# The last block of a cosformer attention + MLP kernel: its first product by seven block products, its units set between halves of the tails' second product

## The chip, the cores and the metric

The kernel runs on one core of a Trainium2 chip. A core has TensorE (PE, with its weight loads as PEld), VectorE (DVE), ScalarE (ACT), GpSimd (POOL) and SyncE (SP), each with a queue of its own, a memory SBUF of 128 partitions, and PSUM, in which TensorE leaves its sums: eight banks of 512 f32 columns. The metric is the time of one execution in microseconds (us) as the device takes it, here the median of a few runs.

## The reference

```python
def phi(x, c, s):
    r = np.maximum(x, 0.0)
    return np.concatenate([r * c, r * s], axis=-1)
q_p, k_p = phi(q, cos_w, sin_w), phi(k, cos_w, sin_w)
kv = np.einsum('bhsf,bhsd->bhfd', k_p, v)
z = np.sum(k_p, axis=2)
num = np.einsum('bhsf,bhfd->bhsd', q_p, kv)
den = np.einsum('bhsf,bhf->bhs', q_p, z)[..., None] + 1e-06
x = (num / den).transpose(0, 2, 1, 3).reshape(B * S, H * D)
h = x @ w_in
g = h * (1.0 / (1.0 + np.exp(-1.702 * h)))
out = g @ w_out
```

q, k and v have 8 batches, 8 heads, 576 positions and 64 features; w_in is 512 x 2048, w_out 2048 x 512. So x has 4608 rows of 512 columns. The function of h is called gelu below; ACT has it as one operation.

## The kernel before

**Blocks.** One batch is a block, b from 0 to 7 (`B` is 8). Its 576 rows of x are 512 main rows, in `x[b]` (columns of x on the partitions in four chunks `kc`, rows along the free axis), and 64 tail rows, which all blocks gather in one tile `xt`. gelu of the main rows goes to four tiles `gT[0..3]` of a pool with five buffers, each with four groups `fc` of 128 columns of h; that of the tails goes to `gt`. The first product h = x @ w_in is made for one `fc` at a time: `mm1` runs four matmuls of 512 columns into one bank of the PSUM pool `pmm` (four buffers of a bank) and ACT's gelu reads it. `wcol(kc, fc)` is the weight: 128 of the columns of w_in with a stride of four. `mm1_tails(fc)` does the same for the 448 tail rows of blocks 1 to 7 together, once, at the end.

**The second product** g @ w_out runs by Winograd's form of Strassen's scheme: rows, the 2048 inner columns and the 512 output columns are cut in two each, and seven block products (`PRODUCTS`, in the order p1 p2 p6 p5 p7 p3 p4) take the place of eight. Each is two halves c of eight matmuls of 256 columns. Three banks are used: w, x and y. p1, p6, p7 and p4 accumulate in x one upon the other, so between two of them x must have been read: p1 and p6 are copied out by ACT (`keep`), p7 is added to the kept p5 on DVE (`join`). p2 goes to w, p5 and p3 to y. The sums of blocks of g (`g_sums`: s1 to s4, each in two calls h of 128x1024) are made on DVE, those of w_out lie ready in `wsum`. For the tails the sums lie in `kr` and `qT`, free by then.

**A block of the loop** (b from 1 on): the 16 `fc` of the first product; meanwhile DVE makes the next block's operands from q, k and v (`trig_q`, two halves for each of five chunks, each chunk then turned by a DMA from SP's queue, `qturn_dma`; `kv_operands`, two `trig` halves for each of nine j, cosine and sine, and a copy of v), and the sums of g. In block 1 the sine halves of the odd j for block 2 are ACT's. At `fc` 14 the next block's kv is made. Then the second product, between whose halves `x_next(nb, c)` makes one chunk of the next block's x: eight matmuls (`num_mm`) into a tile of the PSUM pool `pat` (two buffers of two banks, tile name "at"), three DVE operations (`num_div`: den, inv, xn), and a DMA transpose from SP's queue into `x[nb]` or, for chunk 4, `xt`.

**The last block** (7) has nothing to prepare. Before, it runs: the main rows' first product (L365, gelu L371), `mm1_tails` for all 16 `fc` (L396, gelu L398), the tails' sums and their second product (L507), then the main rows' second product, for which `wino_open(last=True)` gives bank x as two banks, one for each half, and `wino_last` copies and stores each half of p4 by itself. The results of the tails go out by 16 DMAs (`tail_out`), on SP and POOL by turns, those of the main rows by SP.

**Order.** The program is under manual scheduling: each engine's queue holds its instructions in the order in which the code issues them, and an engine waits at an instruction until what it needs has been signalled.

## Time and profile before

| | us |
|---|---|
| median of three runs (281.71 to 282.14) | 281.97 |
| the profiled execution | 282.08 |
| its span, first to last instruction | 280.3 |

The span by stages, from the table of windows (busy time of each engine; the granted TensorE clock is 1.00 in each):

| stage | from, to | PE | DVE | ACT |
|---|---|---|---|---|
| block 6, first product | 197.6, 213.0 | 15.40 | 13.24 | 9.60 |
| block 6, second product | 213.0, 226.2 | 13.20 | 8.99 | 2.35 |
| block 7, main first product | 226.2, 240.0 | 13.80 | 3.46 | 9.55 |
| block 7, tails' first product | 240.0, 252.1 | 12.10 | 3.46 | 8.75 |
| block 7, both second products | 252.1, 276.7 | 24.60 | 8.09 | 5.45 |

A line of the timeline gives start, length, engine, line of the code, operation, what is written from what, shape and count, and in brackets the idle time before it with what ended it. A line of groups gives count, busy time and the mean of one in ns. A line of the chain gives start, length and what the end of the execution waited for then. The length of a matmul in these lines includes the passage through the array; the pace is the start of one to the start of the next.

### The profile page before, as it was taken

To read this page: it belongs to the slowest core of one execution; us is meant where nothing else is said; L and a number is where in the kernel's file an instruction comes from. 1 tells how busy PE (TensorE), PEld (TensorE's weight loads), DVE (VectorE), ACT (ScalarE), POOL (GpSimd) and SP (SyncE) were. 2 spreads that over 40 slices of the span, in tenths; PEclk is the share of its full clock that TensorE was granted. 3 is DMA by queue.
4 is the path that set the end of the run, shared out by engine and by line. 5 is a ranking of instruction groups with operands and counts; after the bars stand their busy time and mean duration, and the time that the engine had idled before them with its cause. 6 is when DMAs were issued, how large, how long until landed. Compare 5 with 4: busy or idle time off the path is not lost.

```text
span 280.3 us, 6580 instructions
## 1 busy us (share of the span) xinstructions
PE 271.2 (97%) x2700; PEld 190.0 (68%) x2700; DVE 184.5 (66%) x450; ACT 130.6 (47%) x230; POOL 41.4 (15%) x70
## 2 busy tenths in 40 slices
PE   7899999999989999999999999999999999999994
PEld 2685645847965588558955895589658965568884
DVE  4843676786893986987598759875987612416111
ACT  6967552677116511652166215621562146772221
POOL 5690002300130012100110012002200120000320
PEclk9999999999999999999999999999999999999999
DMA  7999999999789998999799979968991430000243
GB/s 236 250 210 298 275 281 163 342 325 187 198 147 370 165 205 225 316 170 202 203 324 173 196 187 366 178 183 134 370 221 22 103 112 2 0 0 2 54 135 112
DMA packets 73661, 53.57 MB, mean 191 GB/s; under 512 B 52736, under 2 KB 63488, under 8 KB 73632
## 3 DMA queue, kind: packets, MB, share of 16 engines
q1 hardware_dynamic: 67504, 36.97, 59.8%
q0 software_dynamic: 6128, 16.19, 20.9%
q8 instruction: 21, 0.34, 0.6%
q14 instruction: 8, 0.07, 0.1%
HBM read 36.70 MB, written 9.44 MB: 165 GB/s over the span
## 4 chain that ended last, share of the span: by engine, by line
PE 81%; DMA 11%; DVE 4%; SPq 1%; ACT 1%; issue 1%; POOL 0%; DVEq 0%
PE mm L507 34%; PE mm L365 31%; DMA kf<-in_k_dram 8%; PE mm L396 4%; PE mm L419 4%; PE at L237 3%; PE at L310 3%; DMA sums<-in_v_dram 2%; DVE kr L169 2%; PE mm L388 1%; PE mm L205 0%; ACT kr L167 0%; DVE vt L193 0%; SPq L219 0%; DVE sums L474 0%
## 5 line engine op out<-in xcount | busy, mean ns | idle before, releaser
L365 PE MATMUL mm<-xT,w_in 128*128 128x512 bf16 (+1 forms) x592 | 113.9, 349 | 1.6 <-DMA xT<-xn 1.2
L371 ACT ACTIVATE g<-mm 128x512 bf16<-128x512 f32 x128 | 75.1, 598 | 38.9 <-PE mm L365 38.9
L365 PEld LDWEIGHTS <-w_in 128*128 128x128 bf16 x592 | 60.1, 113 | 48.6 <-issue 2.1
L507 PEld LDWEIGHTS <-sums 128*128 128x128 bf16 x448 | 42.3, 98 | 4.7
L513 POOL DMA_DIRECT2D out_dram<-ysb x24 | 17.5, 729 | 158.3 <-DVE inv L323 96.1
L507 PE MATMUL mm<-wsum,sums 128*128 128x256 bf16 x336 | 40.1, 272 | 0.0
L507 PEld LDWEIGHTS <-g 128*128 128x128 bf16 x336 | 32.2, 98 | 3.8
L169 DVE TENSOR_SCALAR kr<-kf,cosw 128x256 bf16<-128x256 f32 x69 | 23.8, 350 | 9.8 <-DMA kf<-in_k_dram 9.8
L325 DVE TENSOR_TENSOR xn<-at,inv 128x512 bf16<-128x512 f32 x39 | 27.0, 691 | 1.3
L507 PE MATMUL mm<-w_out_sb,g 128*128 128x256 bf16 x224 | 26.4, 272 | 0.0
L169 DVE TENSOR_SCALAR kr<-kf,sinw 128x256 bf16<-128x256 f32 x64 | 21.7, 339 | 0.0
L522 ACT ACTIVATE kept_p<-mm 128x512 f32<-128x512 f32 (+1 forms) x17 | 9.7, 572 | 21.5 <-PE mm L507 21.4
L185 DVE TENSOR_SCALAR qn<-qf,cosw 128x512 bf16<-128x512 f32 (+1 forms) x33 | 16.3, 494 | 2.2 <-DMA qf<-in_q_dram 2.2
L522 ACT ACTIVATE kept_u<-mm 128x512 f32<-128x512 f32 (+1 forms) x9 | 4.9, 550 | 26.7 <-DVE xn L325 16.8
L574 ACT ACTIVATE ysb<-mm 128x512 f32<-128x512 f32 x6 | 3.6, 598 | 29.5 <-PE mm L507 29.5
L310 PEld LDWEIGHTS <-qT 128*128 128x128 bf16 x312 | 14.3, 97 | 3.3 <-issue 1.0
L310 PE MATMUL at<-kvs,qT 128*128 128x65 bf16 x312 | 15.7, 193 | 0.8 <-DVE kvs L245 0.8
L321 DVE TENSOR_SCALAR den<-at 128x8 f32<-128x8 f32 x36 | 5.9, 163 | 15.8 <-PE at L310 15.8
L185 DVE TENSOR_SCALAR qn<-qf,sinw 128x512 bf16<-128x512 f32 (+1 forms) x33 | 15.6, 473 | 0.0
L474 DVE TENSOR_TENSOR sums<-g 128x1024 bf16<-128x1024 bf16 x14 | 9.2, 681 | 8.8 <-ACT g L371 8.8
L470 DVE TENSOR_TENSOR sums<-g 128x1024 bf16<-128x1024 bf16 x14 | 9.6, 687 | 7.9 <-ACT g L371 7.8
L419 PE MATMUL mm<-w_out_sb,g 128*128 128x512 bf16 x64 | 14.8, 379 | 0.0
(120 smaller groups left out, 266.2 us busy)
## 6 DMA issues: line engine op xcount, KB each, us to landing
kf<-in_k_dram SPq DMA_DIRECT2D x6, 1152.0 KB, 6.6
vf<-in_v_dram SPq DMA_DIRECT2D x6, 1152.0 KB, 11.4
qf<-in_q_dram SPq DMA_DIRECT2D x6, 1024.0 KB, 6.8
out_dram<-ysb POOLq DMA_DIRECT2D x24, 256.0 KB, 6.7
w_out_sb<-in_moe_w_out_dram POOLq DMA_DIRECT2D x4, 512.0 KB, 17.5
kf<-in_k_dram POOLq DMA_DIRECT2D x1, 1152.0 KB, 13.4
vf<-in_v_dram POOLq DMA_DIRECT2D x1, 1152.0 KB, 20.6
w_in<-in_moe_w_in_dram POOLq DMA_DIRECT2D x2, 512.0 KB, 10.1
```

The costliest lines, as they stand in the source:

```text
L169: eng.tensor_scalar(o, i, 0.0, w[:, j:j + 1], op0=MAX, op1=MUL)
L185: nc.vector.tensor_scalar(o, i, 0.0, sc, op0=MAX, op1=MUL)
L310: nc.tensor.matmul(ps[:, h // 4, ds((h % 4) * 65, 65)], qT[:, h, ts(c, 128)], kvs_of(h), start=not eps_too, stop=(not eps_too or h % 4 == ...
L325: nc.vector.tensor_tensor(xn, pv[:, :, :, 0:64], inv.unsqueeze(3).to_broadcast([128, 2, 4, 64]), op=MUL)
L365: nc.tensor.matmul(hp[fc][:, t0:t1], wcol(kc, fc), x[b][:, kc, t0:t1], start=(kc == 0), stop=(kc == KC - 1))
L371: nc.scalar.activation(gT[fc // 4][:, fc % 4], hp.pop(fc), AF.Gelu_apprx_sigmoid)
L396: nc.tensor.matmul(hps[:, 64:B * 64], wcol(kc, fc), xt[:, kc, 64:B * 64], start=(kc == 0), stop=(kc == KC - 1))
L419: nc.tensor.matmul(yp[b, t, c0][:, c0:c1], w, w_out_sb[:, fc, c0:c1], start=(fc == 0), stop=(fc == FC - 1))
L470: tt(o[n], a_blk(1, h), a_blk(1, h + 2), op=ADD)
L507: nc.tensor.matmul(bank[to][c], lhs, rhs, start=opens, stop=(fc == HF - 1), skip_group_check=True)
L513: eng.dma_start(out=dst[:, 2 * i + c0:2 * i + c1, ts(n, HD)], in_=t[:, c0:c1])
L522: nc.scalar.activation(o, i, AF.Identity)
```

## The change

It touches block 6, whose work prepares block 7, and block 7.

In block 7 the first product too runs by the same seven block products, for all main rows, and for half of the `fc` of the tails. x is cut in two by columns (k) and by rows (t), w_in by its rows (k) and its columns (f: `fc` 0 to 7 and 8 to 15). A `Unit` makes two `fc` of either half of f: seven products of four matmuls, 256 columns wide for the main rows (w = 0), 224 for the tails (w = 1). Its steps p come in the order 1 2 6 7 5 4 3 and use three banks: A for p1, p6, p7 and p4, one upon the other, Bk for p2, Bp for p5 and p3. p1, p6 and p7 are copied from A to SBUF (`snap`; by ACT in main units, by DVE in tail units), and DVE adds one of these to p2, p5 or p3 (`add`), whose result gelu reads from SBUF; p4's gelu reads A.

The eight banks are laid out by hand as `P8`: 0 to 3 are four tiles of `pmm`, 4 and 5 the halves of one tile of `pat`, 6 and 7 those of another. The tails come first: units of `fc` 0, 1, 8, 9 and of 4, 5, 12, 13 with A in P8[4] and P8[5], Bk P8[6], Bp P8[7], each with four of the other `fc` as `mm1_tails` between its steps, in P8[0..3]. Then four main units, A alternating between P8[4] and P8[5], Bp between P8[7] and P8[3], with three halves of the tails' second product between the steps of each (its w, x, y are P8[1], P8[0], P8[2]), then the two halves left, then the main second product with w P8[6], x P8[4] and P8[5], y P8[7].

The sums of w_in (`win_sum`, s1 to s4, two calls each) are made on DVE in block 6, s1 and s2 after `kv_operands(7)`, s3 and s4 between the chunks of x; those of the tails' x (`x_sum(1, ...)`) after the last chunk, those of the main x after the first tail unit. They lie in kf, vf and qf, the copies and adds in qn, all free by then. Four of the ten `trig_q` halves for block 7 (chunks 3 and 4) and the sine halves of its odd j go from DVE to ACT.

```diff
-    def mm1_tails(fc):
-        hps = pmm.tile([128, MT], F32, name="mm")
+    def mm1_tails(fc, hps):
         for kc in range(KC):
             nc.tensor.matmul(hps[:, 64:B * 64], wcol(kc, fc), xt[:, kc, 64:B * 64],
                              start=(kc == 0), stop=(kc == KC - 1))
...
-    def wino_open(last=False):
+    banks = {"main": {}, "tail": {}}
+
+    def use(which):
+        bank.clear()
+        bank.update(banks[which])
+
+    def give(which, w, x, y):
+        for n, t in (("w", w), ("x", x), ("y", y)):
+            one_bank = not isinstance(t, tuple)
+            two = [t.rearrange("p (c d) -> p c d", c=2)[:, c] for c in range(2)] if one_bank else [
+                u[:, 0:HD] for u in t]
+            banks[which][n] = two
+            banks[which][n, "all"] = t.rearrange("p (c d) -> p c d", c=2) if one_bank else None
+
+    def wino_open():
         for n in ("w", "x", "y"):
-            if last and n == "x":
-                two = [pmm.tile([128, 512], F32, name="mm") for _ in range(2)]
-                bank[n] = [t[:, 0:HD] for t in two]
-                bank[n, "all"] = None
-            else:
-                t = pmm.tile([128, 2, HD], F32, name="mm")
-                bank[n] = [t[:, c] for c in range(2)]
-                bank[n, "all"] = t
+            t = pmm.tile([128, 2, HD], F32, name="mm")
+            bank[n] = [t[:, c] for c in range(2)]
+            bank[n, "all"] = t
...
+    ws = {}
+    for t, names in ((kf, ("s1", "s2")), (vf, ("s3", "s4"))):
+        both = t.rearrange("p i e -> p (i e)")[:, 0:2048].bitcast(BF16).rearrange(
+            "p (n k f) -> p n k f", n=2, k=2)
+        for i, n in enumerate(names):
+            ws[n] = both[:, i]
+    xs_all = qf[:, 0:2048].bitcast(BF16).rearrange("p (w n k t) -> p w n k t", w=2, n=4, k=2)
+    xs = [{n: xs_all[:, w, i] for i, n in enumerate(("t3", "t1", "t2", "nt4"))} for w in range(2)]
+    slots = [qn.rearrange("p c h f -> p (c h f)").bitcast(F32)[:, ts(i, 512)] for i in range(5)]
+    slots.append(qf[:, 2048:2560])
+    slot_no = [0]
+
+    def slot(n):
+        slot_no[0] += 1
+        return slots[slot_no[0] % 6][:, 0:2 * n].rearrange("p (f t) -> p f t", f=2)
+
+    def win_sum(n, i):
+        tt = nc.vector.tensor_tensor
+        o = {m: ws[m][:, :, ts(i, 512)] for m in ws}
+        a = {(0, k): w_in_t[i][:, ts(k, 2), :] for k in range(2)}
+        a.update({(1, k): w_in_t[2][:, ts(k, 2), ts(i, 512)] for k in range(2)})
+        if n == "s1":
+            tt(o[n], a[1, 0], a[1, 1], op=ADD)
+        elif n == "s2":
+            tt(o[n], o["s1"], a[0, 0], op=SUB)
+        elif n == "s3":
+            tt(o[n], a[0, 0], a[1, 0], op=SUB)
+        else:
+            tt(o[n], a[0, 1], o["s2"], op=SUB)
+
+    def x_blk(w, b, k, t):
+        if w == 0:
+            return x[b][:, ts(k, 2), ts(t, 256)]
+        return xt[:, ts(k, 2), 64:B * 64].rearrange("p k (b a t) -> p k a b t", a=2, t=32)[:, :, t]
+
+    def x_sum(w, b, n):
+        tt = nc.vector.tensor_tensor
+        o = dict(xs[w])
+        if w:
+            o = {m: o[m][:, :, 0:(B - 1) * 32].rearrange("p k (b t) -> p k b t", t=32) for m in o}
+        if n == "t3":
+            tt(o[n], x_blk(w, b, 1, 1), x_blk(w, b, 0, 1), op=SUB)
+        elif n == "t1":
+            tt(o[n], x_blk(w, b, 0, 1), x_blk(w, b, 0, 0), op=SUB)
+        elif n == "t2":
+            tt(o[n], x_blk(w, b, 1, 1), o["t1"], op=SUB)
+        else:
+            tt(o[n], x_blk(w, b, 1, 0), o["t2"], op=SUB)
+
+    class Unit:
+        def __init__(self, w, b, u, A, Bk, Bp, act):
+            self.w, self.b, self.u, self.act = w, b, u, act
+            self.n = 256 if w == 0 else (B - 1) * 32
+            self.A, self.Bk, self.Bp = [t[:, 0:2 * self.n].rearrange("p (f t) -> p f t", f=2)
+                                        for t in (A, Bk, Bp)]
+
+        def mm(self, to, a, t, opens):
+            for j in range(2):
+                fc = 2 * self.u + j
+                for k in range(2):
+                    if isinstance(a, str):
+                        lhs = ws[a][:, k, ts(fc // 4, 512)].rearrange("p (f c) -> p f c", c=4)[:, :, fc % 4]
+                    else:
+                        lhs = wcol(2 * a[1] + k, 8 * a[0] + fc)
+                    if isinstance(t, str):
+                        rhs, o = xs[self.w][t][:, k, 0:self.n], to[:, j]
+                    else:
+                        rhs, o = x_blk(self.w, self.b, *t)[:, k], to[:, j]
+                        if self.w:
+                            o = o.rearrange("p (b t) -> p b t", t=32)
+
+                    nc.tensor.matmul(o, lhs, rhs, start=(opens and j == 0 and k == 0), stop=(k == 1),
+                                     skip_group_check=True)
+
+        def g_of(self, f, t):
+            if self.w:
+                return gt5[:, ds(8 * f + 2 * self.u, 2), t, 1:B].rearrange("p f b t -> p f (b t)")
+            return gT[2 * f + self.u // 2][:, ds(2 * (self.u % 2), 2), ts(t, 256)]
+
+        def gelu(self, f, t, i):
+            nc.scalar.activation(self.g_of(f, t), i, AF.Gelu_apprx_sigmoid)
+
+        def add(self, i, j):
+            o = slot(self.n)
+            nc.vector.tensor_tensor(o, i, j, op=ADD)
+            return o
+
+        def snap(self, i):
+            o = slot(self.n)
+            if self.act:
+                nc.scalar.activation(o, i, AF.Identity)
+            else:
+                nc.vector.tensor_copy(o, i)
+            return o
+
+        def step(self, p):
+            if p == 1:
+                self.mm(self.A, (0, 0), (0, 0), True)
+                self.s1 = self.snap(self.A)
+            elif p == 2:
+                self.mm(self.Bk, (0, 1), (1, 0), True)
+                self.gelu(0, 0, self.add(self.s1, self.Bk))
+            elif p == 6:
+                self.mm(self.A, "s2", "t2", False)
+                self.s2 = self.snap(self.A)
+            elif p == 7:
+                self.mm(self.A, "s3", "t3", False)
+                self.s3 = self.snap(self.A)
+            elif p == 5:
+                self.mm(self.Bp, "s1", "t1", True)
+                self.gelu(1, 1, self.add(self.s3, self.Bp))
+            elif p == 4:
+                self.mm(self.A, (1, 1), "nt4", False)
+                self.gelu(1, 0, self.A)
+            else:
+                self.mm(self.Bp, "s4", (1, 1), False)
+                self.gelu(0, 1, self.add(self.s2, self.Bp))
...
     def kv_operands(b):
         for j in range(NS):
-            trig(kr, kf, j, act="sin" if b == 2 and j % 2 else False)
+            trig(kr, kf, j, act="sin" if b in (2, B - 1) and j % 2 else False)
         if b > 2:
             vcopy()
...
     for b in range(1, B):
         nb = b + 1 if b + 1 < B else None
+        if nb is None:
+            break
         f0 = 5 if b == 1 else 0
         for fc in range(f0, FC):
             if nb is not None and fc == f0:
                 for c in range(5):
-                    trig_q(c)
+                    trig_q(c, act=(nb == B - 1 and c > 2))
                     qturn_dma(c)
             if nb is not None and fc == f0 + 1 and b > 1:
                 kv_operands(nb)
+                if nb == B - 1:
+                    for n in ("s1", "s2"):
+                        for i in range(2):
+                            win_sum(n, i)
 
...
                         x_next(nb, c2)
                         if c2 == 3 and nb + 1 < B:
                             load_kv(nb + 1)
+                        if nb == B - 1 and c2 in (1, 2):
+                            win_sum("s3", c2 - 1)
+                        if nb == B - 1 and c2 in (3, 4):
+                            win_sum("s4", c2 - 3)
+                        if nb == B - 1 and c2 == 4:
+                            for n in ("t1", "t2", "t3", "nt4"):
+                                x_sum(1, nb, n)
...
-            continue
-        for fc in range(FC):
-            mm1_tails(fc)
-            if fc == 0:
-                g_sums(("s1", "s2", "s4"), 1)
-        for h in range(2):
-            g_sums(("s1", "s2"), h, TAIL)
-        g_sums(("s3",), 0, TAIL)
-        g_sums(("s3",), 1, TAIL)
-        wino_open()
-        for p in range(7):
-            for c in range(2):
-                wino_mm(p, c, TAIL)
+
+
+
+    b = B - 1
+    two = [pat.tile([128, 2, 512], F32, name="at") for _ in range(2)]
+    P8 = [two[i // 2][:, i % 2] for i in range(4)] + [pmm.tile([128, 512], F32, name="mm") for _ in range(4)]
+    P8 = [P8[i] for i in (4, 5, 6, 7, 0, 1, 2, 3)]
+    full = iter(range(1000))
+    for v_ in (0, 2):
+        unit = Unit(1, b, v_, P8[4 + v_ // 2], P8[6], P8[7], act=False)
+        rest = [2 * v_ + 2, 2 * v_ + 3, 2 * v_ + 10, 2 * v_ + 11]
+        for p in (None, 1, 2, None, 6, None, 7, 5, None, 4, 3):
+            if p:
+                unit.step(p)
+            else:
+                mm1_tails(rest.pop(0), P8[next(full) % 4])
+        if v_ == 0:
+            for n in ("t1", "t2", "t3", "nt4"):
+                x_sum(0, b, n)
+        g_sums(("s1", "s2", "s3"), v_ // 2, TAIL)
+    for qd in range(4):
+        gT[qd] = gpool.tile([128, 4, MT], BF16, name="g")
+    give("tail", P8[1], P8[0], P8[2])
+    use("tail")
+    halves = iter([(p, c) for p in range(7) for c in range(2)])
+
+    def tail_half():
+        p, c = next(halves)
+        wino_mm(p, c, TAIL)
+        if c == 1:
             wino_after(None, p, end=True)
-            if p == 1:
-                g_sums(("s4",), 0, TAIL)
-                g_sums(("s4",), 1, TAIL)
-        wino_open(last=True)
-        for p in range(7):
-            for c in range(2):
-                wino_mm(p, c)
-                if p == 6:
-                    wino_last(b, c)
-            wino_after(b, p, end=True)
+        if (p, c) == (0, 1):
+            g_sums(("s4",), 0, TAIL)
+            g_sums(("s4",), 1, TAIL)
+
+    for u in range(4):
+        unit = Unit(0, b, u, P8[4 + u % 2], P8[6], P8[7 - 4 * (u % 2)], act=True)
+        for p in (1, 2, None, 6, None, 7, 5, None, 4, 3):
+            if p:
+                unit.step(p)
+            else:
+                tail_half()
+        if u in (1, 3):
+            for n in ("s1", "s2", "s3", "s4"):
+                g_sums((n,), u // 2)
+    for _ in range(2):
+        tail_half()
+    give("main", P8[6], (P8[4], P8[5]), P8[7])
+    use("main")
+    for p in range(7):
+        for c in range(2):
+            wino_mm(p, c)
+            if p == 6:
+                wino_last(b, c)
+        wino_after(b, p, end=True)
```

## The prediction

> **What bounds the kernel now.** I read the page's first part, then the chain of waits in order of time, then the timeline of the last two blocks, then the groups with shapes kept apart. Times are us.
>
> ```profile
> PE 271.2 (97%) x2700; PEld 190.0 (68%) x2700; DVE 184.5 (66%) x450; ACT 130.6 (47%) x230; POOL 41.4 (15%) x70
> ```
>
> TensorE is busy nearly throughout. The end of the chain (start, length, work) says the same of the part that changes:
>
> ```profile
> 226.36 13.81 PE mm L365 x64
> 240.17 12.11 PE mm L396 x64
> 252.28 24.47 PE mm L507 x224
> 276.75 0.02 issue
> 276.77 0.38 ACT ysb L580
> ```
>
> The last block is one unbroken run of matmuls: 64 main of 512 columns (0.216 each), 64 tail of 448 (0.189), 224 of 256 (0.109), 50.4 in all. So a matmul less is time gained, and a wait of PE is time lost one for one. The timeline (start, length, engine, line, work) gives what such waits are made of:
>
> ```profile
> 222.31 1.17 SPq L354 DMA_TRANSPOSE xt<-xn  x1
> 222.96 0.69 DVE L532 TENSOR_TENSOR ysb<-mm,kept_p 128x512 f32<-128x512 f32 x1 [0.68 <-PE mm L507]
> 224.45 1.91 PE L507 MATMUL mm<-wsum,g 128*128 128x256 bf16 x16
> 226.40 0.60 ACT L574 ACTIVATE ysb<-mm 128x512 f32<-128x512 f32 x1 [4.83 <-PE mm L507]
> 240.01 12.27 PE L396 MATMUL mm<-xt,w_in 128*128 128x448 bf16 x64
> 240.97 0.54 ACT L398 ACTIVATE gt<-mm 128x448 bf16<-128x448 f32 x1 [0.16 <-PE mm L396]
> ```
>
> Four tail matmuls from 240.01 are issued by 240.77 and their gelu starts at 240.97: 0.20 from PE's last issue to the reader. The other direction stands in block 1's timeline, where four sine halves stand in ACT's queue ahead of gelus:
>
> ```profile
> 60.43 1.71 ACT L167 ACTIVATE kr<-kf,sinw 128x256 bf16<-128x256 f32 x4 [0.95 <-DMA kf<-in_k_dram]
> 62.05 3.15 ACT L371 ACTIVATE g<-mm 128x512 bf16<-128x512 f32 x6
> 62.67 3.61 PE L365 MATMUL mm<-xT,w_in 128*128 128x512 bf16 x16 [0.37 <-ACT g L371]
> ```
>
> The first gelu after them ends at 62.65, PE goes on at 62.67 (0.02), and stood 0.37 for want of a bank. Queued gelus start 0.51 apart, sines 0.41. Groups of 205 to 281 (line, engine, work, shapes, count, busy, mean ns):
>
> ```profile
> L532 DVE TENSOR_TENSOR ysb<-mm,kept_p 128x512 f32<-128x512 f32 x3 | 2.1, 688 | 5.3 <-DMA out_dram<-ty 4.6 <-PE mm L507 0.7
> L470 DVE TENSOR_TENSOR sums<-g 128x1024 bf16<-128x1024 bf16 x4 | 2.8, 690 | 4.8 <-ACT g L371 4.8
> L522 ACT ACTIVATE kept_p<-mm 128x512 f32<-128x512 f32 x5 | 3.0, 597 | 6.7 <-PE mm L507 6.7
> L522 ACT ACTIVATE kept_p<-mm 128x256 f32<-128x256 f32 x2 | 0.8, 384 | 0.8 <-PE mm L507 0.8
> ```
>
> An add from PSUM or a half sum is 0.69 of DVE (0.65 in a row), a copy out of PSUM 0.60 of ACT.
>
> **Matmuls saved.** Main: 64 x 0.216 = 13.81 become 4 units x 28 of 256 columns, 112 x 0.109 = 12.24: -1.57. Half the tails: 32 x 0.189 = 6.06 become 2 x 28 of 224 columns, for which no row exists; the line through 256 (0.109) and 512 (0.216) gives 0.096, so 5.37: -0.69. Sum -2.26. The weights are read with a stride, and one such load lasts 0.113 to 0.118, but it overlaps: strided weights with 64 columns (L388) take 2.3/64 = 0.036 per matmul. If loads set the pace at 0.118 nothing is left (-0.04); I take -2.26.
>
> **Waits added in block 6.** (a) ACT. Four Relu halves of q's chunks 3 and 4 now stand before gelu(0), four sines before gelu(1). The row of the former is L183, 0.71, starts 0.62 apart. ACT is free at 198.35 (the ysb, started 197.83), the Relus end the wait at 200.83, gelu(0) runs to 201.43; sines 4 x 0.41 from 201.34, gelu(1) 202.97 to 203.57. PE has four banks: the sixth group would start at 197.74 + 5 x 0.864 = 202.06 and starts at 203.59: +1.5 (bounds 1.0 to 1.9; k itself lands by 199.9, 6.6 after its issue at 193.33, in time). On DVE the moved halves (4 x 0.39 + 4 x 0.27 = 2.6) pay for s1 and s2 of w_in (4 x 0.65 = 2.6), ahead of the sums; uncovered they would hold kv's evacuation, up to 2.6.
> (b) DVE. In the second product s3 and s4 of w_in (4 x 0.65) stand among the divisions, which ends xn of chunk 4 at 223.0 instead of 222.28. Then DVE's queue holds the four x_sums of the tails, which wait for that chunk's transpose to land: issue 223.03 + 2.3 (xt's row; 2.9 at most in xT's) = 225.33. An x_sum of 448: the line from den's 8 elements (0.163) to 1024 (0.69) gives 0.39, 0.37 in a row (bounds 0.3 to 0.65): 226.8. Behind them is the join of p7, which frees bank x for p4: 227.49. PE wanted p4 at 224.61: +2.9 (2.1 to 4.4).
>
> **Waits added in block 7**, each as chain minus PE's own work since the same point; starts in a row are 0.51 apart on ACT (0.45 for 448), 0.65 on DVE (0.58 for 448).
> - W1, second tail unit's p6 waits for DVE's snap of p1. Chain from the end of the first unit's p3: 0.20, add 0.59, x_sums of the main rows 4 x 0.37, three half sums 1.95, snap 0.62, release: 4.87. PE: full tails 2 x 0.76, p1, p2 0.77, and 0.30 of W2: 2.58. Stall 2.29.
> - W2, a unit's p1 waits for the gelu of p4 before it. The tiles "at" hold two banks each, and the changed program's list of instructions shows p1 with an ACT wait though its bank alternates; so I count the tile as one. 0.30 and 1.06 after the two tail units. For a main unit, from the end of p7: 0.2, snap 0.60, add 0.04 + 0.69, gelu11 0.04 + 0.51, gelu10 0.60, release = 2.70; PE p5, half product 0.87, p4, p3 = 2.19: 0.53 for units 1 and 3; unit 2 has a kept copy in between: 1.04.
> - W3, p7 waits for ACT's snap of p6, which stands behind gelu00, which waits for add12 on DVE. Behind add3 and gelu01 of the unit before, this gives 0.37 in units 1 and 3. In units 0 and 2 DVE has half sums ahead of add12: three (1.95) and four (2.6). Unit 2, from p3's end: 0.2 + 0.69 + 0.04 + 0.60 + 0.04 + 2.6 + 0.69 + 0.04 + 0.51 + 0.60 + 0.03 = 6.04, PE 1.04 + 3 x 0.44 + 2 x 0.87 = 4.10: 1.94. Unit 0 in the same way 1.23. Tail units 0.09 each.
> - W4, the last p4: its second half writes the tile whose other bank ACT is reading for wino_last: 0.2 + 0.38 + 0.03 = 0.61.
> Together 2.29 + 0.30 + 1.06 + 0.53 + 1.04 + 0.53 + 0.37 + 1.94 + 0.37 + 1.23 + 0.18 + 0.61 = 10.45. Where tiles don't count as one it is some 0.6 less.
>
> The gelus of sums read SBUF, for which the rows differ:
>
> ```profile
> L183 ACT ACTIVATE qn<-qf,sinw x2: 707/708/708, 35.8 to 37.1; 128x512 bf16<-128x512 f32 x1, 64x512 bf16<-64x512 f32 x1
> L191 ACT ACTIVATE vt<-vf x2: 1157/1162/1167, 40.7 to 66.8; 128x1152 bf16<-128x1152 f32 x2
> ```
>
> Both read SBUF. The line of the PSUM rows (256: 0.384, 512: 0.598) gives 1.13 at 1152, beside 1.16, so SBUF as such is not slower and 0.60 holds; at 0.71 the three gelus in each chain would add some 1.1. [...]
>
> **Sum.** The profiled execution took 282.08, span 280.3 and 1.78 around it; the median of the runs is 281.97. 282.08 - 2.26 + 1.5 + 2.9 + 10.45 = 294.7, or 294.6 on the median's scale. What follows p4's last half (ACT 0.38, SP's issue, 2.1 to land) stays; the tails' 16 stores are issued before the main product as now, their wait on POOL and SP has nothing of PE behind it.
>
> **Rivals.**
> - R1, cover holds, faster: between p6 and p7 lies half a product, 0.87, against 0.2 + 0.60 + 0.02 for a snap, so one evacuation by itself is hidden. If what stands ahead in the queues were hidden too, only W4 stays: 282.08 - 2.26 + 0.6 = 280.4. It decides where all waits stay below 2.26, a sixth of mine. Against it: the bursts of 3.4, 1.95 and 2.6 on DVE are ahead of the snaps and adds in the list of instructions. 5%; 2% for an even result.
> - R2, only DVE's bursts count, the chains through ACT overlap better than I add them: 282.08 - 2.26 + 2.9 + 2.29 + 1.23 + 1.94 + 0.61 = 288.8. For it: ACT is at 47%. 15%.
> - R3, strided loads pace the shorter matmuls: +2.2, 296.9. 8%.
> - R4, PE slows after its pauses. At the start nine warm matmuls of 512 columns take 3.7, 0.41 each, against 0.216 later. Two such spells, after the pauses of 2.9 and 2.3, lose 1.8 each: 298.3. The table of the slices shows full granted clock, also at that start. 8%. [...]
> The forecast has the remaining 62%.
>
> **How the numbers follow.** The bounds above (-0.5/+0.4, -0.8/+1.5, -0.6/+1.1, and up to a microsecond for hops) put the likeliest at 292.5 to 297.5; the 8-in-10 range reaches toward R2 and R4: 290.5 to 298.3. Within 0.2% (0.56, about what a measurement can tell from no change): 2%; faster 5%; slower 93%.
>
> **What would show it.** PE's idle time in the last two blocks near 15, released by "ACT g" in block 6's first product (1.5), by DVE ysb before block 6's p4 (2.9), by a DVE copy before the second tail unit's p6 (2.3), by ACT before p1 and p7 of the main units. PE's busy time down by 2.3; 0.6 between the last two halves. Wrong if PE idles less than 8 there, or if 224- and 256-column matmuls with w_in run at over 0.115.

## The result, and the profile after

| | before | after |
|---|---|---|
| median, us | 281.95 | 296.51 (six runs, 294.32 to 297.73) |
| ratio, 95% interval | | 1.0509 (1.0476 to 1.0542) |
| the profiled execution | 282.08 | 296.94 |
| its span | 280.3 | 294.8 |
| block 6, from its first matmul to block 7's | 28.57 | 32.87 |
| block 7, to the end of the last copy of `wino_last` | 50.95 | 60.68 |

The change costs 14.6 us, 5.1%. In the profiled executions the two blocks account for 4.30 + 9.73 of it; block 6 starts 0.50 later, and 0.36 more lies outside the span: 14.89, against 296.94 - 282.08 = 14.86. The ratio leaves out executions over 1.5% above the fastest of their kernel (one of 286.47 of the kernel before); the medians hold all. The first part of the page of the changed kernel (busy time, share of the span, instructions):

```profile
PE 272.5 (92%) x2751; PEld 197.3 (67%) x2772; DVE 204.0 (69%) x482; ACT 139.2 (47%) x250; POOL 41.5 (14%) x70
```

TensorE was busy 97% and is busy 92% (the page shows 2751 matmuls beside 2772 weight loads; most of the missing records lie ahead of block 6). What it stands for is in the timeline of TensorE of the changed kernel, block 6 first (start, length, line, work; in brackets the idle time before it and what ended it):

```profile
204.00 7.93 PE L365 MATMUL mm<-xT,w_in 128*128 128x512 bf16 x35 [1.06 <-ACT g L371]
229.26 1.91 PE L515 MATMUL mm<-wsum,g 128*128 128x256 bf16 x16 [2.60 <-DVE ysb L540]
241.70 0.60 PE L665 MATMUL at<-qf,kf 128*128 128x224 bf16 x4 [2.02 <-DVE qn L686]
242.10 1.70 PE L395 MATMUL mm<-xt,w_in 128*128 128x448 bf16 x4
247.48 1.03 PE L665 MATMUL at<-xT,w_in 128*128 128x256 bf16 x8 [0.51 <-ACT gt L674]
252.09 0.60 PE L665 MATMUL at<-qf,vf 128*128 128x256 bf16 x4 [1.40 <-ACT qn L684]
262.37 1.03 PE L665 MATMUL at<-xT,w_in 128*128 128x256 bf16 x8 [0.92 <-ACT g L674]
267.29 0.60 PE L665 MATMUL at<-qf,vf 128*128 128x256 bf16 x4 [1.71 <-ACT qn L684]
290.23 1.03 PE L515 MATMUL at<-wsum,g 128*128 128x256 bf16 x8 [0.47 <-ACT ysb L588]
```

They are, in this order: the queue of Relu and sine halves on ACT (a); the join of p7 behind the x_sums (b); W1; then W2 and W3 of main units 0 and 2; and W4. The idle time in brackets is 0.16 less than what a pause costs, since a matmul's length in these lines is that much longer than its pace (0.38 against 0.216 for 512 columns, 0.27 against 0.109 for 256): in a row each starts 0.16 before the end of the one ahead of it. I call this 0.16 the drain, and count a pause from the point where TensorE would have gone on at its pace: 2.60 in brackets is 2.76.

The chain of waits of the changed kernel (start, length, work) shows what the two longest consist of:

```profile
224.88 2.28 DMA xt<-xn
227.18 0.40 DVE qf L637
...
228.60 0.61 DVE ysb L540
229.26 1.91 PE mm L515 x16
...
237.63 0.43 DVE qf L637
...
239.18 0.61 DVE kr L469
239.82 0.69 DVE kr L471
240.51 0.60 DVE qT L473
241.11 0.55 DVE qn L686
241.70 0.60 PE at L665 x4
```

First the transpose of the tails' last chunk (2.28), the x_sums that waited for it in DVE's queue (L637 and, left out, three more), the join (L540), and only then p4's matmuls. Then the x_sums of the main rows, three half sums of the tails (L469 to L473) and the snap (L686) that TensorE wants.

The fourth line of the timeline is one that the sum doesn't have: four matmuls of 448 columns in 1.70, where they take 0.92 elsewhere. The table of windows of the changed kernel says why (from, to, length, then busy time and count of PE, PEld, DVE, ACT, POOL, then the granted clock, DMA share, GB/s):

```profile
240.00:242.00 2.00, 0.30 (x4) 0.30 (x4) 1.90 (x4) 0.00 (x0) 0.00 (x0) 1.00 0.00 0
242.00:244.00 2.00, 2.00 (x10) 1.04 (x9) 0.97 (x2) 1.18 (x3) 0.00 (x0) 0.51 0.00 0
244.00:246.00 2.00, 2.00 (x11) 1.37 (x10) 1.25 (x2) 0.40 (x2) 0.00 (x0) 0.63 0.00 0
```

Behind W1's pause the granted clock is about one half until some 245.5 (0.63 over the second window is a half for 1.5 of its 2 us). From 242.10 to 246.04 TensorE does what takes 2.28 at its usual pace: 1.66 lost. I call this a spell. The six executions sort by it: 294.3 and 295.1 at mean clocks of 0.999 and 0.998, 296.1 to 297.1 at 0.992 and 0.993, and 297.7 at 0.985. One such spell takes 3.4 x 0.5 / 295 = 0.006 from the mean clock, so these are as much as none, one and two. (The mean also counts the time behind the last matmul, where a low clock costs nothing: in e1's profile, below, the clock is 0.50 from 290 to the end at 291.5, and the mean 0.997 for that alone.)

### The profile page after: what moved, and what is told of

Same layout as the page of the kernel before. It is cut to its first block, busy times and chain, and to the rows that moved or that the text cites. A ratio compares the mean times of both kernels' runs of the same rounds, so it can differ in the third digit from the quotient of the medians.

```text
span 294.8 us, 6778 instructions
## 1 busy us (share of the span) xinstructions
PE 272.5 (92%) x2751; PEld 197.3 (67%) x2772; DVE 204.0 (69%) x482; ACT 139.2 (47%) x250; POOL 41.5 (14%) x70
## 4 chain that ended last, share of the span: by engine, by line
PE 76%; DVE 8%; DMA 7%; ACT 5%; issue 3%; ACTq 0%; POOL 0%; DVEq 0%
PE mm L365 31%; PE mm L515 22%; PE mm L418 4%; PE at L515 4%; PE at L665 4%; PE at L237 3%; PE at L310 2%; DMA sums<-in_v_dram 2%; DMA xT<-xn 2%; PE mm L395 2%; DVE qn L678 2%; DVE xn L325 1%; ACT qn L684 1%; DMA kf<-in_k_dram 1%; ACT g L674 1%
## 5 line engine op out<-in xcount | busy, mean ns | idle before, releaser
L365 PE MATMUL mm<-xT,w_in 128*128 128x512 bf16 (+1 forms) x509 | 99.1, 344 | 4.8 <-ACT g L371 2.2
L365 PEld LDWEIGHTS <-w_in 128*128 128x128 bf16 x528 | 52.9, 114 | 44.8 <-issue 4.9
L371 ACT ACTIVATE g<-mm 128x512 bf16<-128x512 f32 x112 | 65.1, 598 | 33.0 <-PE mm L365 32.9
L515 PE MATMUL mm<-wsum,sums 128*128 128x256 bf16 x288 | 34.7, 272 | 0.0
L515 PE MATMUL mm<-w_out_sb,g 128*128 128x256 bf16 x192 | 22.7, 272 | 0.1
L169 DVE TENSOR_SCALAR kr<-kf,sinw 128x256 bf16<-128x256 f32 x60 | 20.6, 344 | 0.0
L321 DVE TENSOR_SCALAR den<-at 128x8 f32<-128x8 f32 x36 | 5.9, 164 | 14.6 <-PE at L310 14.6
L530 ACT ACTIVATE kept_p<-mm 128x512 f32<-128x512 f32 x14 | 8.4, 597 | 16.1 <-PE mm L515 16.0
L530 ACT ACTIVATE kept_u<-mm 128x512 f32<-128x512 f32 x7 | 4.2, 595 | 21.0 <-DVE xn L325 13.5
L515 PE MATMUL mm<-wsum,g 128*128 128x256 bf16 x96 | 11.5, 272 | 2.6 <-DVE ysb L540 2.6
L469 DVE TENSOR_TENSOR sums<-g 128x1024 bf16<-128x1024 bf16 x14 | 9.6, 688 | 3.9 <-ACT g L371 2.4
```

The costliest lines, as they stand in the source:

```text
L169: eng.tensor_scalar(o, i, 0.0, w[:, j:j + 1], op0=MAX, op1=MUL)
L365: nc.tensor.matmul(hp[fc][:, t0:t1], wcol(kc, fc), x[b][:, kc, t0:t1], start=(kc == 0), stop=(kc == KC - 1))
L371: nc.scalar.activation(gT[fc // 4][:, fc % 4], hp.pop(fc), AF.Gelu_apprx_sigmoid)
L469: tt(o[n], a_blk(1, h), a_blk(1, h + 2), op=ADD)
L515: nc.tensor.matmul(bank[to][c], lhs, rhs, start=opens, stop=(fc == HF - 1), skip_group_check=True)
L530: nc.scalar.activation(o, i, AF.Identity)
```

## The experiments

My theory: all of the loss is pauses of TensorE, each made by what stands ahead of one evacuation in an in-order queue (ACT's halves, DVE's bursts, the gelu ahead of a snap, the tile of two banks that counts as one), plus the spells at half clock that the longest pauses set off. The rivals are stated with each. All were run in five rounds beside the kernel before, whose median was 282.3 to 282.5.

| run | what it does | median, us | ratio (95%) | block 6 | block 7 |
|---|---|---|---|---|---|
| after | | 296.51 | 1.0509 (1.0476 to 1.0542) | 32.87 | 60.68 |
| e1_xsum_late | tails' x_sums behind p7's join | 294.37 | 1.0420 (1.0375 to 1.0465) | 30.09 | 59.28 |
| e2_filler | matmuls of no use in W1's pause | 297.14 | 1.0501 (1.0457 to 1.0544) | 32.86 | 59.24 |
| e3_act_spread | ACT's halves one to a group | 296.88 | 1.0487 (1.0448 to 1.0526) | 33.44 | 61.24 |
| e4_bursts | DVE's bursts cut up | 291.37 | 1.0319 (1.0273 to 1.0365) | 34.34 | 54.45 |
| e5_banks | units in tiles of one bank | 297.38 | 1.0522 (1.0478 to 1.0566) | 34.46 | 59.03 |
| e6_order | snap ahead of gelu on ACT | 294.60 | 1.0418 (1.0375 to 1.0462) | 34.49 | 56.55 |
| e8_dve_both | e1 and e4 together | 287.69 | 1.0181 (1.0149 to 1.0213) | 30.10 | 55.03 |
| e7_all | every cause together | 283.92 | 1.0056 (1.0033 to 1.0079) | 28.56 | 52.53 |
| e9_best | e7 with its new waits mended | 281.49 | 0.9964 (0.9940 to 0.9988) | 28.57 | 49.91 |
| e10_tails_full | e9 with the tails' product in full | 281.17 | 0.9965 (0.9940 to 0.9991) | 28.56 | 49.89 |

Block 6 of e3 to e6 and block 7 of after and e3 hold a spell at half clock in the profiled execution, some 1.1 to 1.7 each (e3's and e4's first run on into block 7 by 0.6 and 0.2). So block 7 of other runs is compared with e1's 59.28, which is that of after without one.

### One cause at a time

**e1_xsum_late** leaves the transpose's wait in DVE's queue, but behind the join:

```diff
-                        if nb == B - 1 and c2 == 4:
-                            for n in ("t1", "t2", "t3", "nt4"):
-                                x_sum(1, nb, n)
+                    if s == 9 and nb == B - 1:
+                        for n in ("t1", "t2", "t3", "nt4"):
+                            x_sum(1, nb, n)
```

> The four sums of the tails' x are issued behind the join of p7 instead of ahead of it. Theory (DVE's queue): the wait of block 6's p4 for the join, 2.60 in the changed kernel's trace, goes, and the sums are done before the first tail unit's p1 needs DVE (transpose lands by 227.2, four sums 1.4, first snap at 230 or later), so the execution is 2.3 to 2.7 shorter than the changed kernel's. Rival (the wait only moves): p6 of the first tail unit, which multiplies the sums, or its snap waits instead, and less than 1.0 is gained.

In e1's timeline of TensorE, p4 of block 6 follows without a pause:

```profile
227.30 1.91 PE L515 MATMUL mm<-wsum,g 128*128 128x256 bf16 x16
```

Block 6 falls by 2.78, what (b) was measured at (2.76), and the other waits stay (2.02 for W1's snap, 0.47 at the end). So the place of four instructions in a queue, not their work, made (b): a DMA's landing was charged to an add that had nothing to do with it. The median falls by 2.1. Block 7 of this execution has no spell at half clock, and is the cleanest reading of the prediction's W terms. Its W1 has the same pause as after's, with the usual 0.92 behind it:

```profile
239.75 0.54 PE L665 MATMUL at<-qf,kf 128*128 128x224 bf16 x4 [2.02 <-DVE qn L686]
240.13 0.92 PE L395 MATMUL mm<-xt,w_in 128*128 128x448 bf16 x4
```

**e2_filler** keeps the pause and fills it:

```diff
+            if p == 6 and v_ == 2:
+                for _ in range(8):
+                    nc.tensor.matmul(P8[2], warm[:, 0:128], warm, start=True, stop=True)
             if p:
```

> Eight matmuls of zeros, 512 columns, are put into the pause ahead of the second tail unit's p6 (2.0 idle in the changed kernel's trace), into a bank that the next group overwrites. They compute nothing. Theory (PE's clock falls after that pause): in the changed kernel's trace the clock is 0.50 to 0.53 from 242 to 245 and the matmuls there take twice their time, a loss of some 1.7; with the pause filled the granted clock stays 1.00, the execution is 1 to 2 shorter where the clock had fallen, and the runs lie closer together, near 294.5. Rival (the slow spell comes by itself or from something else): mean clock and times stay as they were, 294.3 to 297.7.

The timeline of e2 has the filler, and behind it the 448-column matmuls at their usual length; the last line is its table of windows for the stretch where after showed 0.51:

```profile
239.50 1.67 PE L986 MATMUL mm<-warm 128*128 128x512 bf16 x7
241.47 0.54 PE L665 MATMUL at<-qf,kf 128*128 128x224 bf16 x4 [0.30 <-DVE qn L686]
241.85 0.92 PE L395 MATMUL mm<-xt,w_in 128*128 128x448 bf16 x4
```
```profile
242.00:244.00 2.00, 2.00 (x16) 1.44 (x14) 1.30 (x3) 1.44 (x3) 0.00 (x0) 1.00 0.00 0
```

The clock stays at 1.00 and block 7 is 1.44 shorter than after's. But e1's profile has the pause of 2.02 unfilled, no spell behind it either, and a block 7 of 59.28 against 59.24 here; so this profile alone doesn't show that the spell followed from the pause. The median doesn't gain either, where 294.5 was expected: four of six executions still have a mean clock of 0.994, which fits one spell each, and the pause of 2.60 in block 6 is still there to set it off. The test of the cause is e8.

**e3_act_spread** issues the eight halves one behind each of groups 2 to 9, and w_in's s1 and s2 behind group 9:

```diff
-                    trig_q(c, act=(nb == B - 1 and c > 2))
+                    if nb == B - 1 and c > 2:
+                        continue
+                    trig_q(c)
                     qturn_dma(c)
...
             mm1(b, fc)
+            if nb == B - 1 and 2 <= fc <= 9:
+                act_half(fc - 2)
```

> The eight halves moved to ACT are issued one behind each of the groups 2 to 9 of block 6's first product instead of four ahead of gelu(0) and four ahead of gelu(1); the sums s1 and s2 of w_in follow group 9. Theory (ACT's queue stands full ahead of the gelus): PE's waits for ACT g in block 6, 0.16 + 1.06 and what stands unmarked, 1.5 in all, fall below 0.3: 1.2 to 1.5 shorter than the changed kernel. Rival (ACT lacks the time in this stage): each group costs 0.51 + 0.41 to 0.62 against PE's 0.86, the waits come back spread over the groups, and less than 0.5 is gained; or DVE's later sums hold back the evacuation of kv by up to 2.6.

TensorE's timeline of e3:

```profile
213.10 0.40 PE L312 MATMUL at<-kvs,qT 128*128 128x65 bf16 x8 [0.86 <-DVE kvs L247]
227.55 3.04 PE L517 MATMUL mm<-wsum,g 128*128 128x256 bf16 x16 [2.60 <-DVE ysb L542]
```

The waits on gelu in the first product are gone, but the wait that this edit's rival named takes their place: DVE's evacuation of kv is late by 0.86. The first product is 0.51 shorter, a third of (a), and the median, 296.88, isn't below after's. It is the price that the prediction named for w_in's sums on DVE without cover (up to 2.6). DVE stands 1.72 for the landing of v ahead of v's copy (2.01 in after), and w_in's sums come behind that copy; TensorE, no longer held by (a), now reaches kv before DVE is through with them. The second line is the half clock again, here behind the pause of 2.60: 16 matmuls in 3.04 that take 1.91.

**e4_bursts** gives the half sums out singly or in pairs, and the main rows' x_sums before the tail units:

```diff
+    for n in ("t1", "t2", "t3", "nt4"):
+        x_sum(0, b, n)
+    todo = {(0, 2): [("s1", 0, TAIL), ("s2", 0, TAIL)], (0, 5): [("s1", 1, TAIL)], (0, 3): [("s2", 1, TAIL)],
...
-        if v_ == 0:
-            for n in ("t1", "t2", "t3", "nt4"):
-                x_sum(0, b, n)
-        g_sums(("s1", "s2", "s3"), v_ // 2, TAIL)
...
                 unit.step(p)
+                for n, h, of in todo.get((u, p), ()):
+                    g_sums((n,), h, of)
```

> The sums of the main x go ahead of the tail units, and the half sums of g are spread over the main units, one or two behind an add, instead of three or four in a row. Theory (bursts in DVE's queue): the wait of 2.02 before the second tail unit's p6 goes with the slow clock behind it, and the p7 waits of units 0 and 2 (1.40 and 1.71) fall to those of units 1 and 3 (0.2): some 4.5 shorter, 6 where the clock had fallen. Rival (ACT's chain sets those waits, DVE's bursts lie beside it): the p7 waits of units 0 and 2 stay above 1.0 and only the 2.0 with its clock is gained.

W1 and both long p7 waits are gone from e4's timeline; p1's waits stay (0.93, 0.39, 0.92, 0.43 in brackets). Block 7 is 54.45, 4.83 less than e1's, where W1 and the two p7 waits are 2.18 + 1.21 + 1.86 = 5.25. The timeline has the second tail unit's p6 and unit 2's p7 without a bracket, and the pause in block 6, which stays, with its spell:

```profile
229.25 3.43 PE L515 MATMUL mm<-wsum,g 128*128 128x256 bf16 x16 [2.60 <-DVE ysb L540]
241.18 0.55 PE L665 MATMUL at<-qf,kf 128*128 128x224 bf16 x4
262.54 0.60 PE L665 MATMUL at<-qf,vf 128*128 128x256 bf16 x4
```

**e5_banks** exchanges the tiles: the units in tiles of one bank, the tails' second product in those of two.

```diff
-    give("tail", P8[1], P8[0], P8[2])
+    give("tail", P8[6], P8[4], P8[5])
-        unit = Unit(0, b, u, P8[4 + u % 2], P8[6], P8[7 - 4 * (u % 2)], act=True)
+        unit = Unit(0, b, u, P8[u % 2], P8[2], P8[3 + 4 * (u % 2)], act=True)
-    give("main", P8[6], (P8[4], P8[5]), P8[7])
+    give("main", P8[2], (P8[0], P8[1]), P8[3])
```

> Main units and the main second product get the four tiles of one bank (A P8[0] and P8[1], Bk P8[2], Bp P8[3] and P8[7]; x P8[0] and P8[1], w P8[2], y P8[3]), the tails' second product the tiles of two banks. Theory (the chain through ACT sets p1's and p7's waits together, the shared tile only decides at which of the two PE stands): the waits of main units' p1 (0.51, 0.38, 0.92, 0.43) go, those of p6 and p7 grow by nearly as much, and only the 0.47 between the last halves of p4 is gained, 0.4 to 0.8 in all. Rival (the shared tile costs by itself): the p1 waits go and nothing comes instead, 2.2 + 0.5 = 2.7 gained.

The timeline of e5:

```profile
267.46 0.60 PE L665 MATMUL mm<-qf,vf 128*128 128x256 bf16 x4 [2.44 <-ACT qn L684]
273.49 1.03 PE L515 MATMUL at<-w_out_sb,qT 128*128 128x256 bf16 x8 [0.73 <-DVE ty L540]
```

Every wait before a main unit's p1 (0.93, 0.37, 0.92 and 0.43 in e1) is gone, and so is the 0.47 between the last halves: a tile of two banks did count as one (W2, W4). But p7's waits grew, in unit 2 from 1.71 to 2.44, and the tails' product now meets its own shared tile (0.73). Block 7 is 59.03, e1's 59.28: taking all five waits away gained 0.25, with the new 0.73 counted against it. The two waits of a unit hang on one chain of ACT and DVE, so most of what is taken from the first comes out at the second.

**e6_order** issues the gelu of a sum behind the next snap, not ahead of it:

```diff
                 self.mm(self.Bk, (0, 1), (1, 0), True)
-                self.gelu(0, 0, self.add(self.s1, self.Bk))
+                late.append((self, 0, 0, self.add(self.s1, self.Bk)))
             elif p == 6:
                 self.mm(self.A, "s2", "t2", False)
                 self.s2 = self.snap(self.A)
+                flush()
```

> ACT's order alone: in a unit the gelu of a sum is issued behind the next copy out of A (gelu00 behind the snap of p6, gelu01 of units 0 and 2 behind the next unit's first snap) and gelu11 behind gelu10. Theory (what PE waits for is ACT standing at a gelu whose sum DVE has not made): the p7 waits (1.40, 0.20, 1.71, below 0.2) fall below 0.3 each although DVE's bursts stay, and p1's waits shrink by a few tenths each: 3 to 4.5 shorter than the changed kernel. Rival (DVE's bursts hold the units up whatever ACT's order): the waits come back at p4 and p3, less than 1.0 gained.

The timeline of e6, at W1 and at unit 2's p7 (1.70 in e1):

```profile
241.43 0.54 PE L672 MATMUL at<-qf,kf 128*128 128x224 bf16 x4 [2.36 <-DVE qn L693]
261.75 0.60 PE L672 MATMUL at<-qf,vf 128*128 128x256 bf16 x4
```

The waits before p7 are gone; seven of 0.17 to 0.71 are left in the main units. Block 7 is 56.55, 2.7 less than e1's, at the same work on every engine: a snap that TensorE waits for stood behind a gelu that nobody was in a hurry for. It is less than the 3 to 4.5 that I had put down, since W1 grew to 2.36 and the bursts on DVE still reach TensorE by other ways (0.71 ahead of unit 2's p5, for an add). The median is only 1.9 below after's; five of its six executions have mean clocks of 0.988 to 0.994.

### Together

**e8_dve_both** is e1 and e4 in one, and a test of the half clock: without an idle time above 1.1 in brackets in blocks 6 and 7 there should be no spell there.

> The two moves on DVE together: the tails' x sums behind the join of p7, the main x sums ahead of the tail units, the half sums of g one or two at a time. No pause above 1.1 is left in PE. Theory: the gains add, 2.6 + 4.5, to some 287.5 where the changed kernel without a fall of the clock takes 294.3 to 295.1; and if the falls come from the pauses of 2.0 and 2.6, the mean clock is 0.997 or more in all runs and these lie within 1 of each other. Rival (falls come by themselves in this program): clocks of 0.993 and below still appear, with times 2 above.

287.69, as expected from the two gains, and its six executions lie within 1.3 us at mean clocks of 0.997 to 1.000; those of after spread over 3.4. The 35 executions of e7, e9 and e10, whose profiles don't have these pauses either, lie at 0.997 or more too. In the profiles of after and of e1 to e6, blocks 6 and 7 hold twelve pauses of 2.0 to 2.6 in brackets, and each of the six spells there begins within 0.6 of the end of one; pauses of up to 1.84 (e5) have none behind them. So the spells in these blocks come from the long pauses and not from the change's other parts.

**e7_all** joins e1, e4, e5 and e6 with a lighter form of e3: only the four Relu halves of q stay on ACT, behind groups 2, 4, 6 and 8, w_in's s1 goes ahead of v's copy and s2 behind it, and one sum of g behind kv's evacuation.

```diff
-            trig(kr, kf, j, act="sin" if b in (2, B - 1) and j % 2 else False)
+            trig(kr, kf, j, act="sin" if b == 2 and j % 2 else False)
+        if b == B - 1:
+            win_sum("s1", 0)
+            win_sum("s1", 1)
...
+            if nb == B - 1 and fc in (2, 4, 6, 8):
+                act_half(fc // 2 - 1)
```

> All together: ACT takes only the four Relu halves of q's chunks, one behind each of groups 2, 4, 6 and 8; w_in's s1 ahead of the copy of v, s2 behind it, g's first s4 behind kv's evacuation; DVE's sums as in the run with both moves; banks and ACT's order as in the two runs on these. Theory (what was lost is waits, and the saving in matmuls is real): all waits of PE in the last two blocks together fall to 1.0 or less, so 282.1 - 2.26 + 0.3 to 1.0 = 280.1 to 280.9, 0.4 to 0.7% below the kernel before. Rival (ACT and DVE lack the time for seven products with their copies and sums): new waits of 2 or more take the place of the old, and it stays at 282 or above.

Block 6 is back at 28.56, so all of (a) and (b) could be hidden. Block 7 isn't: 52.53, and the median misses what I expected by over 3 us. TensorE's timeline of e7 names the new waits, as its rival had it:

```profile
259.40 1.03 PE L515 MATMUL at<-w_out_sb,qT 128*128 128x256 bf16 x8 [1.00 <-DVE ty L540]
263.54 1.91 PE L515 MATMUL at<-wsum,gt 128*128 128x256 bf16 x16 [0.49 <-DVE ty L540]
```

Both are of the tails' second product, whose banks x and y now share a tile with one another. A wait of 0.58 is left ahead of the first tail unit's p6.

**e9_best** gives that product's y the bank beside w, one bank of its own to Bp of all main units, and spreads the main rows' x_sums too (the lines with a minus are e7's):

```diff
-    give("tail", P8[6], P8[4], P8[5])
+    give("tail", P8[6], P8[4], P8[7])
-        unit = Unit(0, b, u, P8[u % 2], P8[2], P8[3 + 4 * (u % 2)], act=True)
+        unit = Unit(0, b, u, P8[u % 2], P8[2], P8[3], act=True)
...
+    todo_x = {(0, 5): ["t1"], (0, 3): ["t2", "t3"], (2, 5): ["nt4"]}
```

> As all together, with what was left of waits there taken on: the tails' y moves beside w (P8[7], P8[6]) away from x (P8[4]), and all main units take Bp P8[3], so that the tails' p3 and p4 no longer wait for the joins of x and y (1.00 and 0.49); the main x sums go one or two behind an add of the tail units instead of ahead of the first snap (0.58). Theory: 2.1 less than all together, 281.5 to 282.2 there where that took 283.9, so even with the kernel before or up to 0.4% below it. Rival (DVE has no room left in the tail units or at p3): waits of 0.5 and more come back elsewhere and it stays above 283.

The first part of e9's page, and the one wait that TensorE's timeline of it still marks in blocks 6 and 7:

```profile
PE 268.7 (96%) x2751; PEld 196.6 (70%) x2772; DVE 204.4 (73%) x486; ACT 137.4 (49%) x246; POOL 41.4 (15%) x70
```
```profile
252.81 0.60 PE L672 MATMUL mm<-qf,kf 128*128 128x256 bf16 x4 [0.18 <-ACT qn L691]
```

The same 2.26 of matmuls are left out as in after. The page's busy time is 2.5 less than before the change, but this page too lacks 21 of 2772 matmuls, nearly all ahead of block 6; block 7 is to be read by itself, before and in e9 (from, to, length, then busy time and count of PE, PEld, DVE, ACT, POOL, then the granted clock, DMA share, GB/s):

```profile
226.20:277.15 50.95, 50.53 (x354) 36.34 (x352) 15.01 (x23) 24.14 (x44) 4.86 (x10) 1.00 0.14 46
227.15:277.06 49.91, 49.19 (x426) 43.06 (x424) 31.62 (x54) 28.99 (x56) 5.41 (x10) 1.00 0.15 47
```

With the waits gone the kernel is faster than before it, if only by 0.4%: 0.9964 (0.9940 to 0.9988). Of the 2.26, 1.04 arrives in block 7; the rest is in small gaps at the joints between groups, of which the timeline marks only the one above, since 0.16 of each, the drain, counts as busy.

**e10_tails_full** asks what half the tails contribute: e9 without the tail units, all 16 groups of the tails in full.

```diff
-    for v_ in (0, 2):
-        unit = Unit(1, b, v_, P8[4 + v_ // 2], P8[6], P8[7], act=False)
...
+    for fc in range(FC):
+        mm1_tails(fc, P8[fc % 4])
```

> As the run before, but the tails' first product is made in full (16 groups of four matmuls of 448 columns, as before the change), without tail units, without the sums of the tails' x and with the main x sums ahead. Theory: 0.69 more of matmuls and 0.2 to 0.4 less of waits, so 0.3 to 0.5 longer than the run before. Rival (the tail units lose more in waits than they save): 0.3 or more shorter.

Neither comes true: 49.89 against 49.91 in block 7, and the same ratio; the medians' 0.3 lies well within the 2 to 2.6 over which each kernel's executions spread. The tails' product runs without a gap here:

```profile
225.81 12.27 PE L395 MATMUL mm<-xt,w_in 128*128 128x448 bf16 x64
```

The tail units' 0.69 of saved matmuls goes into their own gaps, for 16 more instructions on DVE. The main units alone carry the gain.

## Why the prediction was right, and where it fell short

The forecast was 294.6, slower by 12.6; the median is slower by 14.6, inside the range. Without a spell the two blocks are 4.30 + 8.33 = 12.6 longer (block 7 by e1), as forecast. That the total agrees to a tenth is partly luck: block 6 starts between 196.2 and 199.0 in the twelve profiles, though nothing ahead of it was changed. The forecast's terms against the profiled execution of after, and for block 7 that of e1, which has the same block 7 without the spell (each pause is the bracket + 0.16 there):

| step | forecast | after | e1 |
|---|---|---|---|
| 224-column matmul | 0.096 | 0.096 | |
| (a) ACT's queue in block 6 | 1.5 | 1.54 | |
| (b) join behind the x_sums | 2.9 | 2.76 | 0 (moved) |
| W1 | 2.29 | 2.18 | 2.18 |
| W2, second tail unit | 0.30 | 0.33 | 0.34 |
| W2, main unit 0 | 1.06 | 0.68 | 1.09 |
| W2, units 1, 2, 3 | 0.53, 1.04, 0.53 | 0.54, 1.08, 0.59 | 0.53, 1.08, 0.59 |
| W3, units 0 to 3 | 1.23, 0.37, 1.94, 0.37 | 1.56, 0.37, 1.87, 0.31 | 1.21, 0.37, 1.86, 0.31 |
| p7 of the tail units | 0.09, 0.09 | 0.11, in the spell | 0.12, 0.12 |
| W4 | 0.61 | 0.64 | 0.63 |
| all waits of block 7 | 10.45 | 10.26 | 10.43 |
| spell at half clock | 0 (R4: 1.8 each) | 1.66 | 0 |

**Matmuls saved.** Right: the new shapes run at the pace interpolated for them (0.109 for w_in's 256 columns, 0.096) beside loads of 0.114 to 0.117 each in after, so strided loads don't pace them and R3 falls. The test that I named for it, TensorE's busy time down by 2.3, was badly chosen: in blocks 6 and 7 it rose from 28.57 + 50.53 to 28.89 + 51.89, by 1.68. Fourteen pauses lay bare 0.16 of drain each, and the spell adds 1.66: -2.26 + 2.2 + 1.7 = 1.6. In e9, with neither, block 7's is 1.34 less than before, the rest being the drains at its joints.

**Block 6.** Both terms right to 0.15, and by the mechanisms named: e1 removes (b) and nothing else; e3 removes the waits on ACT. The size of (b) is a little luck: it was counted from the modelled end of p3, 224.61, and from where TensorE would have gone on at its pace, 224.45, the same chain gives 3.04; xn of chunk 4 was ready 0.2 earlier than put down. One step failed unseen: the halves moved to ACT were to pay on DVE for w_in's s1 and s2. But DVE stood 2.01 for the landing of v, which the working doesn't have, so most of the 2.6 saved went there, and only (a) hid the sums; e3 laid that bare (0.86), and e7 puts s1 ahead of v's copy.

**Block 7.** The chains held wait by wait. That tiles of two banks count as one was read from the list of instructions; e5 shows it. R1 (cover holds) and R2 (only DVE's bursts count) fall in after: W2, which has no burst ahead of it, is there in full, and moving bursts (e4) leaves it standing. What R1 described takes another order and other banks for nearly the same instructions (the sine halves are back on DVE): e9 is that kernel, at 281.5 against R1's 280.4.

**What fell short** is the term of R4, put at nothing in the sum and at 8%. Its price was right (1.8 against 1.66), its chance too low: pauses of 2.0 and 2.6 in brackets set a spell off, in some executions after the one (after's profile), in some after the other (e4's), in e3's after both. That covers the 1.9 between forecast and median: executions without a spell took 294.3 and 295.1. The 8% was my estimate; it leaned on the full granted clock in the table of slices at the start, where nine matmuls take 0.41 each all the same. In after the spell runs from 242.0 to some 245.5, and six of the twelve pauses of 2.0 to 2.6 named under e8 have none behind them. What pause is the shortest to set one off, and why only some of them do, no run here tells. Nor do pauses explain every low clock: 3 of 27 executions of the kernel before, beside e1 to e8, had a mean of 0.994, with no such pause in its profile, and one of e1 had 0.986 and one of e4 0.985, with one pause of 2.0 or 2.6 each in these kernels' profiles.

## What to carry to other kernels

Where TensorE is busy throughout, a product by fewer matmuls is paid for in evacuations, and what decides is not their sum on ACT and DVE (49% and 73% here, even in the fast version) but what stands ahead of each in its queue: 2.26 us of matmuls saved turned into 14 of waits, and nearly the same work in another order, on other banks, into a gain of 0.8. So write the queue of each evacuating engine out, and put first what TensorE waits for: a copy out of PSUM ahead of the gelu that only a later stage wants, side work singly between them and not in bursts, an instruction that waits for a DMA behind whatever needn't, and no tile of two banks where two users alternate. Here a pause of 2 us of TensorE cost up to 3.7: in after 2.02 idle, and 1.66 in the spell at half clock behind it.

## What the hardware showed that I had not expected

The half clock after pauses of 2.0 and 2.6, above: in after 1.66 lost behind 2.0 of idle time, in e4 1.52 on the first 16 matmuls behind 2.6 (3.43 for 1.91), and none behind the 2.0 in e1's profile. And small waits move rather than vanish: the five on banks that e5 takes away are 0.93 + 0.37 + 0.92 + 0.43 + 0.47 = 3.1 in e1's brackets, and block 7 gained 0.25, since the next wait of the same chain took up most of them, and a new one in the tails' product 0.73.
